# Sharing the attention transposes and V products among three heads instead of two, with a new order of the work

## The chip, the cores and the metric

The kernel runs on one core of a Trainium2 chip. A core has five engines with instruction streams of their own: TensorE (PE, matrix products, into PSUM), VectorE (DVE), ScalarE (ACT), GpSimd (POOL) and SyncE (SP). DMA engines move data between HBM and the on-chip SBUF; here SP and POOL issue the transfers. The metric is the time of one execution on the device in microseconds, as the median of several runs. Before the change it was 1774.65 us (three runs, 1773.49 to 1776.65).

## The reference

Two layers follow each other, twice: a recurrent attention (A) and a gated feed-forward network (B), each on a layernorm of its input with a residual sum. x has 2048 rows of 512; attention has 32 heads of 128, segments of 32 rows and 8 memory rows. All is bf16.

```python
for s in range(n_seg):                                  # 64 segments
    h = concatenate([mem, x[:, s*32:(s+1)*32]])         # 8 + 32 = 40 rows
    q, k, v = h @ Wq, h @ Wk, h @ Wv                    # per head, 512 -> 128
    scores = where(mask, q @ k.T * 128**-0.5, -1e9)     # 40 x 40 per head
    o = softmax(scores) @ v                             # 40 x 128 per head
    o = einsum('bhte,hed->btd', o, Wo)
    mem = o[:, :8]                                      # memory of the next segment
    outs.append(o[:, 8:])

def B(x): return (sigmoid(x @ w_gate) * (x @ w_up)) @ w_down   # 512 -> 1792 -> 512
```

The memory makes the 64 segments of one attention a chain: a segment needs the output of the one before it.

## The kernel before

**Steps.** The first and the second attention run interleaved. They are called jobs 0 and 1, and job 1 runs six segments behind (`LAG`). There are 70 steps (`emit_step`, L872). In 58 of them both jobs are at work and a matmul has 80 columns (two segments of 40 rows); in the first six and the last six only one is.

**Groups.** A step handles its 32 heads in six groups, five of six heads and one of two (`groups`, L512). A group has these stages: Q and K projections, three heads at a time (L949, 128x128 weight blocks against the 80 columns of `hT`); a copy to `qku` on ScalarE; scores (L984); mask, maximum, subtraction, exponential, sum and reciprocal on VectorE and ScalarE (L998 to L1012); the scaling into `pb` (L1015); the transposes of P (L1027); the copies that spread P^T into `ptsb` (L1032, issued at L1303 to L1313); the products with V (L1054); a copy to `otsb`; and the output projection (L1072), which adds up over all heads in one PSUM bank. The memory rows of that bank go to the next step's `hT` (L1085).

**Pairs of heads.** `pb` holds P of 80 rows (both jobs' queries) and, for each head, 40 keys at a pitch of 64. One transpose takes two heads, head u and head 16 + u: 80 x 128 in, 128 x 80 out, so that a head's keys lie on partitions 0 to 39 or 64 to 103. The spreading copies write the two heads into a block form: for each job 40 columns for the first head, with zeros below, and 40 for the second, with zeros above. The second copy covers partitions 0 to 103 and multiplies by a mask column `lower`, which is 0 on the first 64 partitions. One product then serves two heads of one job: V of both on 104 partitions as weights, 80 columns moving.

**V.** Rows of V that depend on x alone are computed ahead in big passes (`v_pass`, L739), written to a scratch tensor in HBM and brought into `vsb` (L918). Rows that depend on the memory are computed in the step as strips (`strips`, L863) and copied into `vsb` by DMA through `sst` (L929). A `vsb` tile holds two heads' rows (partitions 0 to 39 and 64 to 103) for 8 units; a step takes two tiles of a ring of three. Each job needs four transfers from scratch and four from the strips, on the SP queue.

**Feed-forward work.** `ffn` (L1127) runs once per block of four segments and job, from weights that POOL streams from HBM (L1166, L1167, L1191). These matmuls (L1174, L1197), the V passes and the layernorm transposes (L699, L1142) lie between the steps' own matmuls on TensorE.

**Order.** A `Planner` holds every task with a duration, its reads and writes, and buffer rings. It walks through modelled time and, on each engine, starts the ready task that comes first in a stored list (`SEQUENCE`). The order that results is the program order on each engine. Weight transfers on POOL also get a wait on a TensorE task that, by the model, ended before their planned start (L1282). Where TensorE's plan shows a gap of over 250 ns, `warm` (L447) puts in matmuls on the tile `hot` whose result nobody reads (L1297).

Of the kernel before, what the change touches and what calls it, by code (L numbers as in the profile page):

```python
# [20 lines left out]
P = 128  # L21
# [15 lines left out]
def mm_ns(n):  # L37
    return max(n / 2.4 + 2.5, 25.0)
# [14 lines left out]

SEQUENCE = r"""
;AsOsC|v+MjR9kLb}pcQnda7Mm$^5zu`zb?3;5sKz{Rmj5^3kR*HD{9a4C$pJ<wZm2fIZR%3?+XgW%;+b65$rzYj7ezK;wS2K8bkq`Ct3fbk0_8QV5#pP1SHH##{@E-}1p8b<v1c8}gL^qmgFuu=_Cmod@|aa)Bo
_(!7P{lowmZu!z=QxF6aTzb03ZNYwxWk94HP+-&b5ixb!rw7D&>->wAKE9p&fnHsC!#^79Oqv~2B~jFF>fB&4f|@_*cWiGdtUO{JV9YkvS4<gWKFzS_m2N;?Sd;nQLM*=$%E@Ib;(0pLg3_$2ZWJ(ljh!wN3NUs6
<5F&caLSK>)P*`J@~qpb;Y8L!JhX#{%taT;x!7FSEohnq5cBOK$g1sMwUcQ%dQwvAU?Yl(>+~FP4KnQw<4ai*m$Ni%@eF8yqWT`P6A}d&x}&%Y^h|Oi|C(c*m<{{{QKwuR?f4x6kfo7q7?!*PRo-`h^KDdYq}rrj
Qe}Cx;@>}6<vsP|nLHGVSR`?Jw!dwJc>$f)ug#YOjpt<QNggkYb%c$1L6x@M+krLbO%Xf*rWkO+VsgIXNF=S2DCNakULR0$_XnH*voY9g`Duym?=Qw1DQ1UX_&&DV1o7hG0of;$A4;6oHhlw3(-pf8u_$o1bCsWI
21H2wjjwk>ULoIcfwFF{{WIEcj}(P;nqh|W3C8W^?du{dVtsLV5j-;}!xpE5oI*H(-glbV!Xba!h~dqyDAH8Q{<?vpAWc@uL6XLV_}9<sCt_Ebk=m*)x3+Egk(=uP&?9cwL@07D#aRVqUGrpVxAd=yf@-RLiGaw6
NTi0vYZiE>0Jz9V9l9#&s)QY*9%mDFs#rqvM~Jhu_^M$OM||BbD$P%yrm;??MzxM}(n_{k35|H0!CF#hXp)ejb%omEhqh525X=MRzlUNqJHuH6gbaZ$g8&B-myDPo);n%pUHGq18&5~(vLdWo1&@32N*wJ)(P!Ig  # L60
YPsPtX;IoB6xc~Wc-NkP>>ENdzqQ+2CUI6{FdjQX`5%7%e&!W})4qbjHvwAFJ>Zu5A!7|={Tvw#<b4noq0Q=={ZkZKZe@GMEs@N?ba$8EB(cfCna5V`*IT<8XDYDd+^`?jTP<-T#4f%fWQ^+l2L$=eOhD&&Tg}A=
o(d^E0S^h*W|xu}v&))cVBD@UZWbc1Zw1IjVQ~PlGMjRS4AKjJ{J-sbNp=pfQ>-3Fk2-(OKqfc3p4Qj^EaLHuzfGs{9-yGY;d|Bx;#_AZWf<bcmcD^q<!SKv7?)hFHT0t%Q~Ob;8{_e5p8zrSM3j^V0UA6l<~K+8
qJ|0!*V%&_xZ?Yt0E*-(4@`PBKC3g~GEF#Bc|~h;7j1f6vH`IflKK?e=%?qkkvn1e5JhaZmOFlU%(5u0Hs>L24q5ucwhWIRX-C>7`rQn3M|q$jy$82}IedzD9{sy@`LTXSJIx~!QtE|YPh__?)`PR4g{$3s1>OV5
kDisZ#>ZOlso}JIu!@-+4!Xa38SYa{?+U=Bw;6sY6p`0LbH$jzPzrKd8tPZb8>Uz42l@9dwuVV2;J3K;Rd^B(QLO9R5o@Y09VHdike@DI^E<U=bp)K*-0_35QfiZphl*TxO*Kp%-e^ReuW6ObA7WMsi5I(MFW{9M
1uT02zVE=EO4@EIlq+WD<vErd+36l7K0Z@Z*FSV7eBIVW&36@5*u!b)pw|%zFj}iUdIXD1mw=5|{@Y!KJZKCqD^E9;$uf^%korHhU|Sh=Q)VdU_0xw<SU`{N#8#>p1|HgLVDlqta#Sh?l!HeP29lT+{K@`K<)Mp6
zA8Vk!f0UN)Mob;xoPeQ?aLl`XB1%3TKxhPkd1ImHK8+?j`l_Hr^fIiYB-k~c;tCC!<C&mOui!UI8wir)o}YA^zjX+T_Md853^_Qm}YAvo8j745^l`jABY;6$TnT{2+Ljr6v@(cC7L<>_*z-AP}(7Ay??OSs-Q8`
bieYOqR?{|n&&_>vmt{iqMTR+A<v)5iI}y9!m>&K>iQhOL|y@J&m0EBNk>GH^K^Z?QVHA_va0h}4*{Ea9t62I)*zXJ7EINdi{geJ$x1Wzfxr{lw{mYqw>T_Hz4cnHMF2;R1XC@VQL(0o1F)JmZO9dgG%zCVRCeu7
3p=-~+tO_ycon*Y6@-0<Ln!$dLO}z|P_(!`@VH>XlC(OE6LeIw)y{`npw!2HKI9v9t&pKXBZq>5Jd3UJ1H<hb04!s+Pf7V7fuXmw@4kGYFE6c7BJMjw=XPdb;8B1xd)odOI-6a9<FJY)Rwk}!ag=AwEwr}t8f!q{
aRtb8k)E}}o!S<cpj(8vjJI3#BM}N8I0s?`Z}=75QO3=rP^nPVA#^D7q;Vi&9T{;ZZIH8g0w6Gmg!+Kj<ca-aR+d>)XWl1BiDwb7xz~-2n*#-c`TgjGC-#l~G6uPi;|XKr=W+`bRu`+=nj{K8h>eL%VFe1ek4#7M
JU?IOJ)AusFVI8M2Zq0BU_1x<hVq!^{^3V!VL&!U&vOa&qBH74T11MaEy}NV1w+R@JqTM&nLl26)?Y(~#-2%Rz&frC^-Xule$T@g_(VrkgzgZEu!FN)NxJ-^d+nX$3!(z5BA`!*TOdvmcIWR5MpuHfxs2Gs6swfj  # L70
q{Ho52dpz2KT_Yy)ra>bx1ZUjA)M%A8nYiYbJ@vT_?keO&`A9qOHUa8g0ZWNP3`^#FSVBP!FgU)r}X6FA>&QW8qtKGR^}>NI&MCpavFu8?>y28LnF`0P?6`$P`I$jX-l@j!_H49T}>@yu_qe|i)>n7Q>|S#Rixw~
vUp*-H2v-mHL~^tYN43C{TKY}Ys7Y!N#|%4*_*xT!t={Y)sM(VOXDz^rE_Q>f}x4ruj%c9EYPFI^3=JA;b#NGq-W;<_@C~T>N^&6-XEF~(86+9{~i#5q5bdn6vF1mJ=#yX{q~DzNVc4^3qQh}Lj;U3DmZbc_7O^A
aO;tvP}@sNkkRhU>943-coTs&RS85wk`B07I$Rhfzk3xrXzrn=?H+2gfSXpkciJ}rHrJa#F>>5L4U1@pTAs}x&^ti4BM`U_c1w!<^4T*(I7-U4#WI%K%uLM^ka7BJ-gJvV%oaRPC-`dp0YI@53!yV(W(Bu;-hqk+
?gY7Ri?#O0Vybj{bLXQx%s5vml24M5`+5n_dwSc$|83*n`|)7ZvXRPSeU5qPOmyjO$AbYRG7mt~8hgQ|Ej7NVJ#*M!bDyI?b1NB@k+WQso&-iW2xY>xpw&`%)Qk@&c|eVHjrnajbCvTHBf6jEiqWy2B79ze8tLW^
Rm^<Q7rDKo?^#9DG=h)jZvB#$SNM_ZHB@AwmtqX1LqyHIcxQrTWvTgKRVLM*E9fcTKn-P}5LEjk*aCxa*uJmvk-&DP8XwO}TYHft!l3)u!;T%fetz4NZGa}EBeg0}n<K3P<V=WeqOgrsDc@u7FB<fomTQUji(l2^
r8rN)bo_gnWSReyFn*DP)QO~52c8C>ep^QTezVeAR^?wRP;fGCo2(^|Ey@J3L6VsyJ=-iDKXpE0)?Ip{jyZq|(uJb@7nGBi=leueOcIe@1MD=;ffKzH+sn|kpf=KW0TLbG5rzcXoq^l(!bGIn5Qo?pnXYJ4m5b)t
V&Xl^1Cdo>gy{^>LyVE{84PiLpza9^s~VP;vj8nyM#^{6klzZNL!<Np+yw)Ft0}m^3B0704|2^N=8b-;p1;MRE9PC7c&b`2h7?&biIx$r<}TIlyQm=^AJj({UU2yu`g<e#j&nvsM7#8gGc(xA0Lk~QgZ!$#GJ^Kv
hw%{Jv-&YY{A_AOcDIpMHn^foOT8G%xUP3!Jx5gKy>lWo6*}y>-|ujubGL`~oM6ZXUjsLxdb^nTM45mPo&+2ONt+8WZrWH3pRTu=GJB?_=dF2f?l{#{K%K+~s=CN@o=OK~X~8+;{29IXcND8wO3Qcj+BSOps~*JE
)IiAPY}L|2(?_FY#$mWq=2(vpVzXW1j6im<nD!~c#r}Is%`-N<>I0k-F^JUrjSpFz8z&$u#XBXv+qxEpN%;^g@EB#|6KwrOKzH!&n54%Atl~PL{GO|d4!wQl(d4FqOaLq$DeZyR0%PkMZki<;JF4|0g5H#?(UKN_
B5t~w{4v;)3H1aZi_jP@61_azKrAqo9yqT_uxHam(oPCqic3^f;ecc?awH$$`vR+BxWaCbD46a+4c+NY(JPgdZ-#G2Q98}020k_M@3xhycCo^}Zm3tLp-~67d$-`lww{bAacv*LfY$Zs6@NzB45n|7uiw!Frux4r  # L80
Vbk09oZ5N0mP~AYyX%F#|G~r<Atf>BV08~aQO1p)l?rgR7GMm%H)dnNKn9vJqOX99$>h>39P26|#`9rW);?dljEkmpM{u2hogN5h;rZZ*Au>p32Q`V$y|t+9Q$W<sqS}QYl{u9esG$#-P8I=;4T@YJjd~_CU3*y4
+CiwW$^1H=@=7|i;w{j-|4+gtXcwa?>n`I!|JrcM6DY{yD-d)RBaJSh<71r4q&0gLqSv`;NMPT~xQA%@iUvs5Siv@?5KV#rtFqAWh4tr`wjHBoI$2UHQ8Lpvtqm#VwJW%J{Yq=LCM*^{kPY5$9Od=&`s(}ZqguH5
u!DDl$u~uz9xYPTH_#7pwTLR!kXwg#5XK`KzJkX{S0{y0dLd)T0zc^0U&aeT!)hgua_8GT_>a-7C<s*c*~}?DF#3_Q>2J#+s8S7-!*DTO3*jx_eMid`9Jnotc8s*q&_iV!t>KYR<1}KKkuNg~$<u&_0Q4y-+Q7=K
h%N)X9196K9ZX1kbKh6Q+J2WO9?xH!g3#(}K{C)YnTJX2g+2z`DlF84q#dTb-8tO!DBAyIb5KKV^qKrII=L^7P9`gSk14=Et{Ep9_7_rlTen3Mu3T`6+IN;ZR`<rx!L(RBukVn^kgOAtXh8OXg}Yh^Bt(mljkb-H
=|Xc?Hzj<5sgLA&M7Pv2Hke=J^|)#kU%4j|<aUj#ez(_8X>T9j{Kv7(-V(C;h1W=bjz`Ka8<o54@E~nNCHZpTv@*LUSc8F}6bM*2Vm?98pIdwI;>c|+b5C1f0!LV)>X&5J%rlOn$PNF#blh#}Wk~cxn(+m3i-`un
%fDaxfsPGl=f;T#qQ^-jzTXRylZ5Gbp*EGz`WrI_mFx?8II}@~qBsSUfOU2$z$14e8p~>$U?1ACt@XijNvtKFdr9}x_csseTr{V%2ta!e;mLEhY)}6uYIbR&gkVV>h}!>+bYeV)!}$(Vi!;>YI%n>JcqQSRVS!ib
xXMw6U)dNTIob8uIiUMbGayImRvtI`lbhk5h*;h&@Vr{K{|vX+Di?yaE&&f->&%8toYize(iQx1w(l{xaKi$pCw!rOo0Wi|$NQJ`smOoW&INHohTt|`t2)5)uy@21FY3)YlzN)^*c(oqfP+EZx)D>X=$QF)5SY5J
3BfVrQqd-d9mp1d+*jiSi#W2Eo3}Oud-~&PpS`LzZ#5s2-KVtHzHReUp9TNB17#X~rp-BeiBEF#-VY-eUQ6Rjp+D`CEJe*n!tq*Lkv}FhCeDV8r$nB>=(h2H23;7tltIg`QJ&AC)U~hf?iy{X4L4E+Su4n!DA87j
u?U}5t~;?7xiC)v%aIca1dS6jR_InzL02buCkiX9Q${=N0q!+fH0WB$tm0CttsJ(esyW;ISr$d#ZlE&hBht^PxYk4L5XWS@Jj5U9-w0I2wVquBO5d;o!((=6K6REWaMIr@$m58J;nkc3$Ty;i@IDcLn-{BpLsvlE
g!)kIRhe&IQW6saRx$yE)N2v8DCV^o6}E9Mb&v}edu~~3Rd6~1$U5PbI74)1_=*k>PVT*mj>Ywra{`@$Ta3Qf@6*emC$KG4FEj>>vuE{IpE*~-wL;5;KzHauJrW%ZgU9l8d2eZ+v?uQzzLL0FK|86Y9&oy;z>juM  # L90
jX?x8E<GN*80{3;=}WRYJYK(19SRX<_GSp#>2_UI80^`sxExP=gL0?^S?S7fyNr4mQKg{Y-8dr~{L!Hf?mKEQcbb$1g|y{H4Bxp0*nGH$ku=E5{Lw-N=ucX<1Rfiy;38f_ewAFV+*2!XyB{-tUJrBeEO_a$uRdEV
T@VqKCldx(iq#N5vLcxiZaDm(JgDR{-{w7?uUTW5&q23MWn7)Z7mQB?coS@!I2h#QcM)_Nk?E;JH_-n?NdUn~#$@yr%I*B86;L><4DoL^p5o_|%{qHCNj^a3wC-OWCH1Yo?x$^UK}X>@AEUMsI<N&@?vYeV9)DiC
bVr$wqJnTzAK=y#R8BW9>(e0sAz%i$wQ(SS8Pka3N<=Eh6o_1$8+I%I$Co%x8j^>m$w>?9#-zkb?MTU2iy>_zEbTNtKjk^O#;-Hn&y&p6F0P8Up-dB^@wyTH&%HmK9;|>6cn5@B4_A7FUI7tG0ZL9bi_8MNR+Lvf
Ve9O8DIwrUXi&d;kbj=XMnUtlv86*vTNG-Kc~;b9QIph(oI%V$<7F@Bz56<2<Q=u#So@>CrTuK#C@4wIT#Kn7*)L1{GdFEbm9l7>f5w4>*guM5J7yd(!~ybSEg&%TE@SuPJZu-Q^I;r-5YTeNCOQV_J+}R1{{8-X
@baQz7MyJaMnfAHG_M@Nl9(lP6PL_?RFJe)JBCdu8;D1@*2~927___0Yn>eW6}b3CBC)fkp@8Di@)Jc)?Bqp9jbXnO%G&Zh9OcwEGV{sRi?sAvhZ}}%S!PFUlWpx<OX^vGLCSbMOL>*zZ_DgSV3Azq!hsYG9A!Sp
YY`FD^0jECcTDlW*^En{9metb#OzYkeV?89>sw`A9V}yzXIA?4B*S5+++k}JElYwDpP&|0^!}tb*nZPB?>WwhvJ^4r0r(G=h-4X?{aqsK_2V*rlFEj9N><^%X!~`dR(`>bscqFn7Z<;!#(_PidPUb))4LpRZlS(F
zfxdR?_f~HC1p;r+-qV|@W~TwX!M(4TaI3^F42u!1mS{xdymvE8QX>hLU1tYBQ(qkV<t~_Ju5vn_Ktx70={M3IZ-8DaIowumHXn8A_p(emJm}Z*INactOMp|i9!}kU}Vpq01MmctRSlq$v2aR^&CcYeYBiF$1`B|
# [1279 lines left out]
```

## Time and profile before

| what | value |
|---|---|
| median of three runs | 1774.65 us |
| profiled execution | 1778.1 us, its span 1776.3 us |
| TensorE busy | 1757.0 us, 40068 matmuls |
| VectorE, ScalarE, GpSimd busy | 1173.7, 1162.7, 576.2 us |
| transposes of P (L1027) | 1120, of 80 columns |
| products with V (L1054) | 2048, of 80 columns |
| copies into ptsb | 840, for 12 per step |
| transfers into vsb from scratch, from strips | 508, 516 |
| TensorE busy from 400 to 1600 us | 1195.98 of 1200 us |

Times in the profile are microseconds from the start of the span unless marked ns. "L949" is a line of the kernel. PEld is TensorE's loading of weights, which overlaps its matmuls; SPq is the queue that issues transfers. A group's row gives busy time and mean duration, then the idle time of its engine ahead of it and what ended that time. A single matmul lasts some 200 ns from start to end, but the next starts long before, so the distance between starts says what one costs. Durations in the prediction come from the profiled execution.

### The profile page before, as it was taken

Reading aid. Unit: us, or ns where it says so; the run is one execution under the profiler, and the core shown is the slowest. Engines: PE = TensorE matmul, PEld = TensorE weight load, DVE = VectorE, ACT = ScalarE, POOL = GpSimd, SP = SyncE. Lnnn points to the kernel's source line nnn. Section 1 sums busy time; section 2 is a strip of 40 time slices with the busy share of each in tenths; the row PEclk is TensorE's granted clock in tenths of the full one; section 3 lists DMA queues with packets and bytes.
Section 4 is the critical chain, followed back from the end, with each engine's and each line's share of the span. In section 5 each row is a group of like instructions: output and inputs, shape, how many; then the busy total and the mean of one; then the engine's idle time right before and its main releaser. Section 6 shows DMA issues by size and latency. Waiting matters only on the chain.

```text
span 1776.3 us, 92287 instructions
## 1 busy us (share of the span) xinstructions
PE 1757.0 (99%) x40068; PEld 1509.3 (85%) x40068; DVE 1173.7 (66%) x4044; ACT 1162.7 (65%) x2998; POOL 576.2 (32%) x833
## 2 busy tenths in 40 slices
PE   9999999999999999999999999999999999999998
PEld 4688788889888888989898898989888888889886
DVE  4376676777566567756776677657766766666675
ACT  6676767676666656766666667666666666666664
POOL 5413032513333242323334241333324232333432
PEclk9999999999999999999999999999999999999999
DMA  9835354734555464545556453555546444554543
GB/s 350 277 88 156 84 161 139 208 95 134 160 161 157 130 183 133 143 131 162 162 144 182 132 165 111 154 156 168 154 131 190 124 138 129 162 153 136 170 132 108
DMA packets 135289, 273.43 MB, mean 154 GB/s; under 512 B 30826, under 2 KB 68594, under 8 KB 134882
## 3 DMA queue, kind: packets, MB, share of 16 engines
q0 software_dynamic: 56512, 182.57, 35.1%
q1 hardware_dynamic: 78370, 84.96, 16.6%
q8 instruction: 314, 5.14, 1.3%
q14 instruction: 93, 0.76, 0.1%
HBM read 221.78 MB, written 27.07 MB: 140 GB/s over the span
## 4 chain that ended last, share of the span: by engine, by line
PE 93%; DMA 2%; DVE 2%; issue 1%; POOL 1%; ACT 1%; SPq 0%; POOLq 0%; ACTq 0%; DVEq 0%
PE bank L949 32%; PE bank L1072 16%; PE bank L1174 11%; PE bank L739 8%; PE bank L863 7%; PE bank L1197 5%; PE bank L984 4%; PE bank L1054 4%; PE bank L1027 2%; PE bank L699 1%; PE bank L1297 1%; DMA vsb<-sst 1%; PE bank L1142 1%; DMA wd<-in_B_w_down_dram 0%; POOL wu L1167 0%
## 5 line engine op out<-in xcount | busy, mean ns | idle before, releaser
L949 PE MATMUL bank<-hT,wq_sb 128*128 128x80 bf16 (+3 forms) x8960 | 615.5, 198 | 2.0 <-issue 1.5
L949 PE MATMUL bank<-hT,wk_sb 128*128 128x80 bf16 (+3 forms) x8960 | 614.8, 198 | 0.0
L1311 ACT CAST qku<-bank 128x480 bf16<-128x480 f32 (+4 forms) x770 | 387.6, 506 | 216.9 <-PE bank L949 179.5
L949 PEld LDWEIGHTS <-wq_sb 128*128 128x128 bf16 x8960 | 452.1, 99 | 22.7 <-issue 12.1
L949 PEld LDWEIGHTS <-wk_sb 128*128 128x128 bf16 x8960 | 446.8, 99 | 0.0
L998 DVE TENSOR_TENSOR st<-bank,cst 40x240 f32<-40x240 f32 (+3 forms) x768 | 278.0, 367 | 167.3 <-PE bank L984 160.3
L1072 PE MATMUL bank<-otsb,wo_sb 128*128 128x80 bf16 (+1 forms) x8960 | 359.9, 198 | 1.2 <-ACT otsb L1311 1.0
L1072 PEld LDWEIGHTS <-wo_sb 128*128 128x128 bf16 x8960 | 335.1, 99 | 15.8 <-issue 2.6
L1166 POOL DMA_DIRECT2D wg<-in_B_w_gate_dram x217 | 164.4, 757 | 310.4 <-PE bank L1174 102.6
L1311 ACT CAST otsb<-bank 128x480 bf16<-128x480 f32 (+3 forms) x420 | 198.5, 483 | 67.3 <-PE bank L1054 45.6
L1167 POOL DMA_DIRECT2D wu<-in_B_w_up_dram x217 | 163.7, 755 | 218.5 <-PE bank L984 81.0
L1191 POOL DMA_DIRECT2D wd<-in_B_w_down_dram x217 | 153.7, 708 | 209.1 <-PE bank L984 71.2
L1008 ACT ACTIVATE st<-st 80x240 f32<-80x240 f32 (+3 forms) x420 | 158.6, 381 | 35.5 <-DVE st L1005 32.5
L1010 DVE TENSOR_REDUCE small<-st 80x6 f32<-80x240 f32 (+3 forms) x420 | 150.9, 362 | 32.8 <-ACT st L1008 31.1
L1174 PE MATMUL bank<-xnT,wg 128*128 128x128 bf16 (+2 forms) x1784 | 171.6, 218 | 0.4 <-DMA wg<-in_B_w_gate_dram 0.4
L689 POOL TENSOR_TENSOR small<-small,cst 128x1 f32<-128x1 f32 (+1 forms) x80 | 44.6, 559 | 391.6 <-DVE small L688 386.6
L1174 PE MATMUL bank<-xnT,wu 128*128 128x128 bf16 (+2 forms) x1784 | 171.0, 218 | 0.0
L984 PE MATMUL bank<-qku 128*128 128x80 bf16 (+1 forms) x2240 | 162.3, 198 | 0.7 <-ACT qku L1311 0.7
L1005 DVE TENSOR_TENSOR st<-st,small 80x240 f32<-80x240 f32 (+3 forms) x420 | 153.9, 369 | 4.0
L1015 DVE TENSOR_TENSOR pb<-st,small 80x240 bf16<-80x240 f32 (+3 forms) x420 | 152.9, 369 | 3.8
L1003 DVE TENSOR_REDUCE small<-st 80x6 f32<-80x240 f32 (+3 forms) x420 | 151.1, 362 | 4.4
L1054 PE MATMUL bank<-ptsb,vsb 104*128 104x80 bf16 x2048 | 136.5, 199 | 3.5 <-DMA vsb<-sst 1.0
(106 smaller groups left out, 2396.2 us busy)
## 6 DMA issues: line engine op xcount, KB each, us to landing
wg<-in_B_w_gate_dram POOLq DMA_DIRECT2D x220, 256.0 KB, 4.3
wu<-in_B_w_up_dram POOLq DMA_DIRECT2D x220, 256.0 KB, 4.4
wd<-in_B_w_down_dram POOLq DMA_DIRECT2D x220, 256.0 KB, 4.3
vsb<-scr SPq DMA_DIRECT2D x460, 48.0 KB
vsb<-sst SPq DMA_DIRECT2D x464, 32.0 KB
scr<-vst SPq DMA_DIRECT2D x112, 96.0 KB
wv_sb<-in_A_Wv_dram SPq DMA_DIRECT2D x8, 512.0 KB
wo_sb<-in_A_Wo_dram SPq DMA_DIRECT2D x10, 384.0 KB
```

The source lines that it names most:

```text
L949: nc.tensor.matmul(o_ap, lhsT=W[:, c, h * P:(h + 1) * P], rhs=mv(c), start=(c == 0), stop=(c == DC - 1))
L984: nc.tensor.matmul(s_all(SB)[:, w0 + i, :], lhsT=fview(qku[:, i, 0, 0:1], [(1, P)]), rhs=qku[:, i, 1, 0:ncol], start=True, stop=True)
L998: pl.add("DVE", dve_ns(n, True), lambda gsz=gsz, hs=hs, st=st, SB=SB, pj_=pj_, npj_=npj_, mk=mk, idx=idx: nc.vector.tensor_tensor(out=st[p ...
L1005: pl.add("DVE", dve_ns(n), lambda gsz=gsz, hs=hs, st=st, mx=mx: nc.vector.tensor_tensor(out=st[pr, hs], in0=st[pr, hs], in1=mx[pr, hs].uns ...
L1008: pl.add("ACT", act_ns(n), lambda hs=hs, st=st: nc.scalar.activation(out=st[pr, hs], in_=st[pr, hs], func=ACTF.Exp, scale=self.scale), r=s ...
L1054: nc.tensor.matmul(fview(OB[:, o:o + 1], [(ncol, 2), (1, L)]), lhsT=self.vsb[halves[u // 8]][0:64 + L, j, (u % 8) * P:(u % 8 + 1) * P], rh ...
L1072: nc.tensor.matmul(WB[:, c * ncol:(c + 1) * ncol], lhsT=self.wo[:, h, c * P:(c + 1) * P], rhs=otsb[:, hl, 0:ncol], start=(h == 0 and c == ...
L1166: pl.add("POOL", 760, lambda wg=wg, fs=fs: nc.gpsimd.dma_start(out=wg[:], in_=self.wgv[:, :, fs]), r=[("wo", self.H - 1)], w=[gk] + bt, la ...
L1167: pl.add("POOL", 760, lambda wu=wu, fs=fs: nc.gpsimd.dma_start(out=wu[:], in_=self.wuv[:, :, fs]), r=[("wo", self.H - 1)], w=[uk] + bt, la ...
L1174: nc.tensor.matmul(gu[:, 2 * i + k, 0:n], lhsT=W[:, c, i * P:(i + 1) * P], rhs=xnT[:, c, rw], start=(c == 0), stop=(c == DC - 1))
L1191: pl.add("POOL", 760, lambda wd=wd, ip=ip: nc.gpsimd.dma_start(out=wd[:], in_=self.wdv[:, 2 * ip:2 * ip + 2, :]), w=[dk] + (["boot"] if se ...
L1311: nc.scalar.copy(out=dst, in_=src)
```

## The change

**Triples.** Heads 0 to 23 form eight units of three (u, 8 + u, 16 + u), heads 24 to 31 four units of two. The groups are now four with two triples (six heads), one with three pairs and one with one pair. `pb` has a pitch of 40, so a transpose takes 120 or 80 adjoining columns, and three heads' keys lie on partitions 0 to 119. The spreading copies are three for a group of triples, the second and third with mask columns `third[1]` and `third[2]`. A product of a triple has 120 partitions and 120 columns, of a pair 80 and 80.

**V tiles.** A step now takes one tile A (triples, 8 units) and one tile B (pairs, 4 units, half the width), from a ring of two each. Rows have a pitch of 40, so there are no gaps to clear. Each job needs five transfers from scratch and five from the strips, three of 8 heads and two of 4.

**Loads.** Wq, Wk and Wo are cut to suit the new groups; the first group needs nine heads of Wq and Wk.

**Order.** There is a new `SEQUENCE`. A second stored list, `TURNS`, fixes the order in which tasks take the `qku` buffers. The planner's constants change: 120 ns from a task to POOL, 465 ns (before, 205) after a TensorE task for the pace of weight transfers, 5.1 us (before, 4.7) for a weight transfer's landing, 114 ns (before, 80) for one small instruction.

**Places.** `hot` becomes part of `otsb[1]`, `negh` part of `small`.

```diff
+    TO_PE, TO_POOL, PACE = 32.0, 120.0, 465.0
...
+    def in_turn(self, pool):
+        own = [b.users[0] for b in self.bufs if b.users and b.pool is pool]
+        turn = [own[q] for q in unpack(TURNS, len(own))]
+        for a, b in zip(turn, turn[2:]):
+            self.tasks[b].deps.add(a)
...
-        for u in range(0, self.HH, 3):
-            us = list(range(u, min(u + 3, self.HH)))
-            self.groups.append(([h for k in us for h in (k, self.HH + k)], us))
+        for us in ((0, 1), (2, 3), (4, 5), (6, 7), (8, 9, 10), (11,)):
+            self.groups.append(([h for u in us for h in self.unit(u)], us))
...
+    def unit(self, u):
+        return [u, 8 + u, 16 + u] if u < 8 else [16 + u, 20 + u]
...
-        self.NV = 3
+        self.NV = 2
-        self.vsb = [c.tile([P, 2, 1024], BF16, name=f"vsb{i}") for i in range(self.NV)]
+        self.vsb = {("A", i): c.tile([P, 2, 1024], BF16, name=f"vsb{i}") for i in range(self.NV)}
+        self.vsb.update({("B", i): c.tile([P, 2, 512], BF16, name=f"vsb{self.NV + i}") for i in range(self.NV)})
-        self.pb = [c.tile([LW, HG, 64], BF16, name=f"pb{i}") for i in range(3)]
-        self.ptsb = [c.tile([P, HG, 2, L], BF16, name=f"ptsb{i}") for i in range(3)]
+        self.pb = [c.tile([LW, HG, L], BF16, name=f"pb{i}") for i in range(3)]
+        self.ptsb = [c.tile([P, 17 * L], BF16, name=f"ptsb{i}") for i in range(3)]
+        self.hot = fview(self.otsb[1][:, 0, 0:1], [(1, P)])
...
-        halves = [self.nxt("vsb", self.NV) for _ in range(2)]
+        vt = self.nxt("vsb", self.NV)
+        slots = [(("A", vt), i, 8 * i, 8) for i in range(3)] + [(("B", vt), i, 24 + 4 * i, 4) for i in range(2)]
...
-            for i4 in (0, 2, 1, 3):
+            for vh, i, h0, nh in slots:
...
+            w = gsz // nu
-                    nc.tensor.transpose(out=pt[:, ul * LW:(ul + 1) * LW], in_=pb[full, 2 * ul:2 * ul + 2, :].rearrange("p i k -> p (i k)"),
+                    nc.tensor.transpose(out=pt[:, ul * LW:(ul + 1) * LW], in_=pb[full, w * ul:w * ul + w, :].rearrange("p i k -> p (i k)"),
                                         identity=self.ident[full, full])
-            for i in (0, 1):
+            for i in range(w):
...
-                        nc.tensor.matmul(fview(OB[:, o:o + 1], [(ncol, 2), (1, L)]),
-                                         lhsT=self.vsb[halves[u // 8]][0:64 + L, j, (u % 8) * P:(u % 8 + 1) * P],
-                                         rhs=ptsb[0:64 + L, ul * nj + idx, :, :], start=True, stop=True)
+                        nc.tensor.matmul(fview(OB[:, o:o + 1], [(ncol, w), (1, L)]),
+                                         lhsT=self.vsb[vh][0:w * L, j, u % 8 * P:(u % 8 + 1) * P],
+                                         rhs=ptsb[0:w * L, 3 * L * (ul * nj + idx):3 * L * (ul * nj + idx) + w * L], start=True, stop=True)
...
-        ends = [tk.start + tk.dur + self.pl.LAT["PE"] for tk in pes]
+        ends = [tk.start + tk.dur + self.pl.PACE for tk in pes]
```

## The prediction

> **What bounds the kernel now.** I read the page's engine shares first, then the chain that ended last, then its pieces in order of time, then the groups by form, then the timeline of a step with one job.
>
> ```profile
> span 1776.3 us, 92287 instructions
> PE 1757.0 (99%) x40068; PEld 1509.3 (85%) x40068; DVE 1173.7 (66%) x4044; ACT 1162.7 (65%) x2998; POOL 576.2 (32%) x833
> PEclk9999999999999999999999999999999999999999
> ...
> PE 93%; DMA 2%; DVE 2%; issue 1%; POOL 1%; ACT 1%; SPq 0%; POOLq 0%; ACTq 0%; DVEq 0%
> ```
>
> TensorE is busy for 99% at full granted clock, and the chain runs through it for 93%. VectorE and ScalarE have about 600 us of room each. So the price of an edit is what it does to TensorE's row of matmuls, and next to that what it does where TensorE has nothing to do. Pieces of the chain (start us, us, what) give the rhythm:
>
> ```profile
> 603.14 0.22 PE bank L1054 x6
> ...
> 606.98 0.89 PE bank L1174 x16
> ...
> 612.61 0.86 PE bank L949 x24
> ...
> 617.34 0.11 PE bank L1027 x3
> ```
>
> 24 matmuls of 80 columns take 0.86 us, 35.8 ns each; 16 of 128 columns (L1174) take 0.89, 55.6 each: 0.41 ns a column and some 2.5 ns each. Transposes (L1027) and products with V (L1054) keep that rhythm (36.7 in both, rounded). Weight loads are hidden behind the matmul before them. The groups of loads by form (busy us, mean ns) show one more thing:
>
> ```profile
> L1054 PEld LDWEIGHTS <-vsb 104*128 104x128 bf16 x2048 | 102.7, 98 | 18.6 <-issue 6.4 <-DMA vsb<-scr 0.2
> L1027 PEld LDWEIGHTS <-pb 80*128 80x128 bf16 x1120 | 69.1, 98 | 15.4 <-DVE pb L1015 2.0 <-DVE st L998 0.4
> L776 PEld LDWEIGHTS <-xvl 128*64 128x64 bf16 x64 | 3.3, 109 | 3.4 <-ACT wd L1311 0.4 <-issue 0.4
> L863 PEld LDWEIGHTS <-xvl 128*32 128x32 bf16 x64 | 1.5, 96 | 1.9 <-issue 0.4 <-ACT xvl L1311 0.2
> L1197 PEld LDWEIGHTS <-hff 128*96 128x96 bf16 x14 | 1.3, 122 | 2.0 <-DVE hff L1180 1.2 <-issue 0.4
> ```
>
> A load of 32 columns takes 96 ns, of 64 109, of 96 122: 0.41 ns a column. One of 128 columns takes 98, no more than one of 32. Full loads are fast, short ones pay for every column.
>
> **Part one, the transposes.** A step transposed 16 pairs; it will transpose 8 triples and 4 pairs, always with 80 columns moving. Over 70 steps 280 of 1120 go: 280 x 35.8 ns = 10.0 us less, all of it on the path.
>
> But the stationary operand of a transpose is P itself, and its width falls from 128 columns (two heads at a pitch of 64) to 120 or 80. By the slope a load of 120 columns streams for 120 x 0.41 = 50 ns, and the 80-column matmul before it covers 33. The trace has one such place: at 1755.74 us a 96-column load (40 ns) follows a matmul of the 25 ns rhythm, and the matmul behind it lasts 396 ns where the next lasts 379: 17 ns stick out, as the sum says. I count 17 ns for the second triple of each group, which follows the first. The first follows other work: over the timeline 59% of the runs of transposes stand behind 80 columns, 29% behind 128 or 512 (0 exposed), the rest behind shorter ones (25 ns): 12.6 ns on average. 70 x 4 groups x (17 + 12.6) = 8.3 us more. The 80-column loads of the pairs stream 33 ns and stay covered. Bounds: 0 if such loads are hidden, 14 us if each shows 25 ns. I take 8.3, since the 96-column case is nearest.
>
> The Trainium skill speaks against the change here: "TensorE: Matmul & The Clock Gate", section on weight-path perf modes, says that the fast load is on only with 128 weights of a type other than FP32. Its section on LDWEIGHTS prices a plain load at columns / 1.2 ns, 100 ns for 120 columns; by that estimate the exposed time would be some 34 us and the kernel would end near 1793 us. The rows above agree with the first and show half of the second, 0.41 ns a column.
>
> **Part two, the products with V.** Per job and step 16 matmuls of 80 columns become 8 of 120 (120 x 0.41 + 2.5 = 52.5 ns) and 4 of 80. 128 job-steps x (16 x 35.8 - 8 x 52.5 - 4 x 35.8) = 128 x 9.6 ns = 1.2 us less. Only the fixed part is saved. Their loads stay 128 wide.
>
> **Part three, spreading P into the block form.** A group of six heads in triples has one plain and two scaled copies of 160 elements for one and one of 240. From the rows of the copies (ScalarE 459, 360, 325 ns scaled and 347, 246, 213 plain for 240, 120, 80; VectorE 331, 270, 247 and 268, 205, 184): 160 elements take about 392 and 280, and 289 and 226. Mixed as now, 0.73 us becomes 0.97: +0.24 us x 232 groups, and +0.23 x 48 groups with one job, 67 us over both engines. Other TensorE work covers it at 65% use; without that cover 67 us would be the price, and where TensorE waits for this group alone it is some 0.2 us.
>
> **Part four, ten transfers for eight.** The strips' issues (median 587 ns on SP) and those from scratch (355 ns) grow by two each in a full step: 1.9 us more of SP's 25 us. Behind them queue the scratch writes, x loads and stores. SP waits 349 us in all for L1054 before L918, because three half buffers hold one and a half steps; two whole sets hold two, so the same queue loses much of that wait. In a full step I price this at nothing: the first product stands some 9 us behind its strips (L863 at 609.59, L1054 at 620.63). In a step with one job it shows:
>
> ```profile
> 107.09 1.91 PE L863 MATMUL bank<-wv_sb,hT 128*32 128x512 bf16 x32
> ...
> 109.66 3.55 SPq L929 DMA_DIRECT2D vsb<-sst  x4
> ...
> 112.61 0.65 PE L1297 MATMUL bank<-hot 128*128 128x512 bf16 x3
> ...
> 113.21 0.97 PE L1297 MATMUL bank<-hot 128*128 128x512 bf16 x4
> ...
> 114.34 0.38 PE L1054 MATMUL bank<-ptsb,vsb 104*128 104x80 bf16 x6 [0.16 <-issue]
> ```
>
> Filler matmuls (L1297) stand where nothing useful is ready, and the first product waits for the strips of the first half, two issues. Now it waits for three, 0.57 to 0.89 us later (four issues in 3.55 us here, two in 1.15 in the next step). Three steps (102 to 136 us) have such fillers: 3 x 0.73 = 2.2 us more. Bounds: 0 if other work is put there, 12 x 0.89 = 10.7 us if all steps with one job pay.
>
> **Edits at nothing.** The gap clears (three of 1.89 us on ScalarE) go and the ptsb clears grow, both under the boot's fillers and V passes; uncovered, 5.7 us less to 0.6 more. The first group needs nine heads of Wq and Wk for six, 0.79 MB at 372 GB/s, 2.1 us: those loads are issued from 7 us on and first used at 48; uncovered +2.1. The filler operand moves into otsb1, so a filler can wait for that copy, 0 to 0.36 us (240 elements) at twelve places in the chain. Two reductions for the masks are paid in the boot.
>
> **Part five, the order.** Nothing in the trace shows it. What it can win is TensorE's idle 19.3 us, less 1.0 at the start and 4.8 in the last 16 us, plus 5.6 us of fillers between 85 and 218 us: 19.1 us. What it can lose I bound by 10 us: as much again as the chain loses between 100 and 160 us (fillers 6.4%, issue 4.7%, POOL's weight issues over 6%, so some 17% of 60 us). There the planned landing of weights (4.7 to 5.1 us) and the pace of POOL's issues (205 to 465 ns) act, in the helpful direction. I take a third of the 19.1, 6.4 us less.
>
> **Sum.** -10.0 + 8.3 - 1.2 + 2.2 - 6.4 = -7.1 us: 1771.0 for the profiled execution (1778.1, span 1776.3) and 1767.5 against the median of 1774.65, which lies 3.5 below it.
>
> **Rivals.** *Loads hidden:* if loads of 120 columns cost no rhythm, or transposes stand behind long matmuls, 8.3 us come back: 1759.2. For it: 29% already stand so; against it: the 17 ns.
> *The order wins nothing:* -0.7 in all, 1774, no change. For it: the middle of the run (400 to 1600 us) has only 4 us idle.
> *Slower:* the third strip transfer gates the first product in all twelve one-job steps, 10.7 us for 2.2, with no gain of the order: 1774.65 - 2.9 (parts one and two) + 10.7 = 1782.4. It decides above 0.54 us a step ((2.9 + 3.55) / 12), if the order wins nothing. For it: the timeline above; against it: the last six steps show few fillers.
>
> **How the numbers follow.** Forecast with the order's gain 0.45, own range 1761 to 1771; loads hidden, under 1761, 0.17; no change 0.16; slower 0.22. A measurement tells 0.2%, 3.5 us, from nothing. Faster 0.62, same 0.16, slower 0.22. The range of 1757 to 1782 reaches past the hidden loads and to the slower rival, and leaves out about 2 in 10.
>
> **What would show it.** Transposes 840 in number, 560 of their loads 120 wide at about 132 ns, about 52 ns between two triples; 1536 products, 1024 of them with 120 columns; spreads about 67 us dearer; fillers and idle from 85 to 220 us. Loads of 98 ns at 120 columns, or two triples 36 ns apart, refute part one. A changed idle in the middle of the run would make the prediction wrong from the order alone.

## The result, and the profile after

The changed kernel takes 1790.12 us (median of four runs, 1788.38 to 1794.11) where the kernel before takes 1775.35 in the same sitting: 0.8% slower, ratio 1.0082, 95% interval 1.0067 to 1.0097. Forecast were 1767.5 us, a range of 1757 to 1782, and "faster". The profiled execution took 1789.87 us. Its page:

```profile
span 1788.0 us, 91153 instructions
PE 1752.0 (98%) x39103; PEld 1512.2 (85%) x39311; DVE 1182.3 (66%) x4076; ACT 1179.3 (66%) x3243; POOL 578.6 (32%) x837
PEclk9999999999999999999999999999999999999999
...
PE 89%; ACT 3%; DVE 2%; issue 1%; SPq 1%; DMA 1%; POOL 0%; DVEq 0%; ACTq 0%; POOLq 0%
```

TensorE shows 5 us less busy time than before, in a span that is 11.7 us longer, and the chain runs through it for 89% instead of 93%. The records of 208 of its matmuls are missing (39103 for 39311 weight loads), so part of the 5 us may be theirs; but waits did grow. The groups by form (busy us, mean ns of one | idle before them) show the weight loads that the prediction spoke of:

```profile
L1067 PEld LDWEIGHTS <-pb 80*120 80x120 bf16 x560 | 55.7, 134 | 9.6 <-DVE pb L1054 1.9 <-DVE st L1044 0.4
L1067 PEld LDWEIGHTS <-pb 80*80 80x80 bf16 x280 | 22.2, 118 | 4.2 <-DVE pb L1054 0.9
L1096 PEld LDWEIGHTS <-vsb 120*128 120x128 bf16 x1024 | 65.5, 98 | 15.7 <-issue 4.6 <-DMA vsb<-sst 0.3
```

A load of 120 columns takes 134 ns (132 were forecast), and one of 128 columns 98, though it has more rows (120 for 80).

Adding up, for each kind of matmul, the distances from one start to the next in the two traces gives where the path changed (each missing matmul is counted where its weight load stands). Transposes fall from 46.2 us to 41.2, products with V rise from 80.5 to 82.9, V passes from 146.2 to 152.2, and fillers from 25.0 to 30.8 (94 to 129 matmuls); what is left adds some 2 us, and the sum is 11.6 us. The start of each step's strip tells when: the strip of step 1 starts at 89.3 us before and at 97.2 after, 7.9 us late. Up to 1500 us the lag stays mostly between 6 and 10, and the last strip is 11.8 us late. So the boot (all that comes before the first steps) lost 8 us, the long middle gave nothing back, and the end lost a little more.

In the boot two rows of ScalarE's waits stand out (15 to 62 us; us in total, times, longest):

```profile
ACT wg L1354 <- DMA scr<-wg: 5.5, 1, 5.5
ACT wd L1354 <- DMA scr<-wd: 4.7, 1, 4.7
```

The boot copies V rows out of PSUM into a ring of nine buffers (the wg, wu and wd tiles), from which they are written to scratch. ScalarE waits for a buffer whose write has not landed, and the timeline of the second wait (start us, us, engine, what) shows how it reaches TensorE:

```profile
53.03 1.03 PE L778 MATMUL bank<-wv_sb,xvf 128*128 128x512 bf16 x3
...
55.90 0.58 ACT L1354 CAST wd<-bank 128x512 bf16<-128x512 f32 x1 [4.70 <-DMA scr<-wd]
...
56.38 0.59 ACT L1354 CAST wg<-bank 128x512 bf16<-128x512 f32 x1
56.86 0.25 ACT L1354 CAST kx<-bank 128x84 bf16<-128x84 f32 x1
56.98 0.47 ACT L1354 COPY xvf<-bank 128x128 bf16<-128x128 bf16 x1
...
57.51 1.46 PE L778 MATMUL bank<-wv_sb,xvf 128*128 128x512 bf16 x3 [3.45 <-ACT xvf L1354]
```

The copy into xvf is short and ready, but it stands in ScalarE's queue behind the copy that waits. TensorE is idle for 3.45 us for it. Before, the longest such wait of ScalarE was 0.7 us.

The wait has a second price. Two stretches of this time (from and to in us, length, busy us of PE, PEld, DVE, ACT and POOL, granted TensorE clock, DMA share, GB/s), in the changed kernel and then before:

```profile
56.00:58.00 2.00, 0.49 (x2) 0.22 (x3) 0.00 (x0) 1.88 (x5) 0.73 (x2) 0.75 1.05 356
58.00:62.00 4.00, 4.00 (x31) 1.79 (x30) 0.41 (x1) 1.45 (x3) 1.92 (x4) 0.70 0.93 338
```

```profile
56.00:58.00 2.00, 2.00 (x19) 1.07 (x18) 0.52 (x1) 1.17 (x2) 1.12 (x2) 1.00 1.11 307
58.00:62.00 4.00, 4.00 (x22) 1.61 (x24) 0.21 (x1) 2.41 (x5) 1.63 (x3) 1.00 1.03 361
```

From 57.0 to 60.4 us the granted clock is 0.50, and matmuls of 512 columns start some 427 ns apart where they otherwise start 216 apart: 1.4 us more. So of the 6.0 us by which the V passes grew, 4.5 are two waits (3.45 and 1.0 us) and 1.4 this clock.

A step with one job answers to the step that the prediction showed:

```profile
114.65 1.91 PE L902 MATMUL bank<-wv_sb,hT 128*32 128x512 bf16 x32
117.22 4.29 SPq L968 DMA_DIRECT2D vsb<-sst  x5
...
120.60 1.94 PE L1340 MATMUL bank<-otsb 128*128 128x512 bf16 x9
...
122.38 0.48 PE L1096 MATMUL bank<-ptsb,vsb 120*128 120x120 bf16 x6
```

From the strip's start to the first product it is 7.73 us, 7.25 before: 0.5 us more, about what the forecast put on the third transfer. Fillers stand right ahead of the product in both, so whether the transfer or the fillers set it is not shown, and the strips' lag does not grow in these steps (7.9 us at step 1, 7.8 at step 5).

### The profile page after: what moved, and what is told of

The parts are those of the page before. It is cut to its first block, busy times and chain, and to the rows that moved or that the text cites. A ratio compares the mean times of both kernels' runs of the same rounds, so it can differ in the third digit from the quotient of the medians.

```text
span 1788.0 us, 91153 instructions
## 1 busy us (share of the span) xinstructions
PE 1752.0 (98%) x39103; PEld 1512.2 (85%) x39311; DVE 1182.3 (66%) x4076; ACT 1179.3 (66%) x3243; POOL 578.6 (32%) x837
## 4 chain that ended last, share of the span: by engine, by line
PE 89%; ACT 3%; DVE 2%; issue 1%; SPq 1%; DMA 1%; POOL 0%; DVEq 0%; ACTq 0%; POOLq 0%
PE bank L988 32%; PE bank L1114 17%; PE bank L1216 10%; PE bank L902 7%; PE bank L778 6%; PE bank L1023 4%; PE bank L1096 4%; PE bank L1239 4%; PE bank L1067 2%; PE bank L738 1%; DVE st L1037 1%; PE bank L1340 1%; SPq L968 1%; ACT ptsb L1346 1%; PE bank L1184 1%
## 5 line engine op out<-in xcount | busy, mean ns | idle before, releaser
L1354 ACT CAST qku<-bank 128x480 bf16<-128x480 f32 (+3 forms) x770 | 380.7, 507 | 215.5 <-PE bank L988 185.1
L988 PEld LDWEIGHTS <-wq_sb 128*128 128x128 bf16 x8960 | 453.4, 99 | 23.3 <-issue 11.7
L1346 ACT ACTIVATE ptsb<-bank,small 80x160 bf16<-80x160 bf16 (+5 forms) x477 | 169.5, 379 | 27.7 <-PE bank L1067 23.9
L728 POOL TENSOR_TENSOR small<-small 128x1 f32<-128x1 f32 (+1 forms) x80 | 44.8, 563 | 402.1 <-DVE small L727 400.0
```

The source lines that it names most:

```text
L988: nc.tensor.matmul(o_ap, lhsT=W[:, c, h * P:(h + 1) * P], rhs=mv(c), start=(c == 0), stop=(c == DC - 1))
L1346: nc.scalar.activation(out=dst, in_=src, func=ACTF.Copy, scale=by)
L1354: nc.scalar.copy(out=dst, in_=src)
```

## The experiments

All were timed beside the kernel before on one chip per group of runs. That kernel's median moved between 1774 and 1778 us over the groups, so ratios are compared, not times. Line numbers shift by a few lines from kernel to kernel.

**The changed kernel again**, as the measure for its neighbours.

> The changed kernel itself, beside the runs of this call, so that they are read against it on the same chip: 1790 to 1793 us, some 0.8% above the kernel before.

Measured: 1794.3 us against 1777.2, ratio 1.0106 (1.0091 to 1.0120), somewhat worse than in the first sitting. The products' waits for V rows are larger here (4.6 us in the trace for 2.2), which matters below, and the mean granted clock was 0.998 in three of the four runs for 0.999 in all four of the first sitting.

**Full weight loads.** pb's tiles are laid next to constants, so that a load can run eight columns over:

```
-  in_=pb[full, w * ul:w * ul + w, :]           # 120 or 80 columns
+  in_=pbw[:, w * L * ul:w * L * ul + m]        # m = 128 but for a group's third pair
```

> The transposes of P in the groups of three read 128 columns of pb instead of 120 (the eight columns behind a head triple are constants or the next tile's, and the eight extra rows of the result are not read), and two of the three in a pair group read 128 instead of 80. Order, spreads, products and transfers stay. Theory (a weight load of fewer than 128 columns is slow and shows): the 120-column loads, 134 ns each in the changed kernel, become about 108 ns like the full ones, the 560 transposes behind them go from a mean of 52.0 ns to 36 to 41, which is 6 to 9 us less: 1781 to 1784. Rival (the loads lie under other work, and the transposes are spaced by something else): the spacing stays at 50 ns and the time within 2 us of 1790.

Measured: 1788.2 us, ratio 1.0058 (1.0040 to 1.0075). The loads, by form:

```profile
L1071 PEld LDWEIGHTS <-cst 80*128 80x128 bf16 x770 | 57.5, 99 | 15.8 <-DVE cst L1057 3.5 <-issue 0.8
```

With eight columns more a load takes 99 ns in place of 134 (108 were expected). The transposes' sum falls from 41.2 us to 36.7. That sum holds a few long waits; the distances under 200 ns fall from a mean of 47.1 ns to 39.0, which is 6.8 us over 840. In groups of two triples the first shows 50 ns behind 80-column work and 40 behind longer work, and 40 to 42 with full loads; the second shows 55 or 45, and 35 with full loads (medians). So the theory holds for the spacing. By the ratios the time falls by 4.3 us against the first sitting and 8.5 against the second. The profiled execution is the slowest of the six (1795.2 us): its products waited 5.9 us for V rows from the strips, where the first profile of the changed kernel shows 1.8, its V passes 5.5 us for one copy, and the clock was at 0.50 for 6.8 us from 56.2 and for 3.4 us from 1694.6.

**The table's load early.** The removed gap clears were ScalarE's first instructions, so the load of its table came with them at 0.74 us; in the changed kernel it stands in front of the first copies of the V passes.

```
   nc.vector.memset(self.negh, -0.5)
+  nc.scalar.copy(out=self.third[1], in_=self.negh)
```

> The changed kernel with one small ScalarE copy put ahead of everything, so that the load of ScalarE's table (1.28 us, at 0.74 us before and at 13.56 us in the changed kernel, in front of the first copies into xvf) comes early again. Theory (the removed gap clears had carried the table load; the boot passes the delay on): the first V pass starts 1.3 to 1.9 us earlier and the end follows: 1788 to 1789. Rival (what bounds the boot is the transfers, so a late start of the V passes is taken up at the next wait for a buffer): the first V pass is early, step 0 is not, 1790.

Measured: 1800.3 us, ratio 1.0123 (1.0106 to 1.0141), no gain. The first V pass did start earlier (14.21 us in its timeline, 16.44 in the changed kernel), yet the strip of step 0 stood at 73.67 us, against 72.5 and 72.89 in the two profiles of the changed kernel. ScalarE waited longer instead:

```profile
ACT wd L1355 <- DMA scr<-wd: 7.0, 1, 7.0
```

The rival holds: an earlier start is taken up at the next full buffer. That its ratio is even 3 us above the worse one of the changed kernel is in part the clock: its trace has it at 0.50 for 6.8 us from 55.1 (TensorE was idle for the first half of this) and for 3.4 us from 304.2, with waits for V rows of 1.6 and 1.3 us, where the changed kernel's trace has the one stretch of 3.4. The rest was not settled.

**Two more boot buffers.** The order stays as planned; only the ring grows by two halves of a vsb tile.

```
   order = self.pl.plan()
+  self.bootp.tiles = self.bootp.tiles + [self.vsb[("A", 1)][:, i, :] for i in (0, 1)]
+  ...   # buffers dealt out anew, the longest free one first
```

> The changed kernel with eleven instead of nine buffers for the boot's V rows (two halves of a vsb tile that is not used before step 1 join the ring); the order of every engine stays. Theory (ScalarE's waits of 5.5 and 4.7 us at 41 and 56 us are waits for a buffer whose write to scratch has not landed, and TensorE loses 1.0 and 5 us behind them): both waits shrink or go, the strip of step 0 starts 4 to 6 us earlier, time 1784 to 1786. Rival (the transfers as a whole are late, weights included, since the DMA engines are full from 10 to 60 us): the wait moves to the next transfer, and the time stays within 2 us of 1790.

Measured: 1793.7 us, ratio 1.0088 (1.0073 to 1.0103). The boot did as the theory says: V passes lost 2.2 us against their rhythm of 216 ns instead of 6.6, the clock stayed at 1.00, and step 0 started 4.5 us earlier. ScalarE still waits 5.4 and 1.6 us for buffers, but TensorE only 1.5 us behind it. (All seven traces of the new order with nine buffers have the stretch at 0.50 between 55 and 63 us; of the eleven with more, one has such a stretch in the boot, from 43.1 us, with a wait of 3.46 us.) At the end nothing of it was left: the strips' lag grew from 4.5 us at step 1 to 12.9 at the last. By itself the boot's gain does not reach the end. That later waits of the products for V rows take it up is the likely reason (their waits between 290 and 1590 us are 5.9 us here, 1.3 before), not shown by this run alone.

**Pairs in the new order.**

```
   def ptr(...):
+      if w == 3: three transposes of 80 columns; return
   def pvm(...):
+      if w == 3: three products per job, rhs 80 wide; return
```

> The changed kernel with its order, transfers, weight loads and three spreads kept, but in the groups of three triples' work is done as three transposes of 80 columns and products of pairs (80 wide) as before; the products take V rows of the wrong heads, so this prices time alone. Theory (sharing in threes saves some 8 us of TensorE's time, and the loss lies in the order and the boot): transposes 840 x 41 ns for 560 x 52 (+5 us), products 1536 x 37.7 ns for 1024 x 53 (+3 us): 1795 to 1799. Rival (sharing in threes is itself what does not pay): 1788 to 1792.

Measured: 1798.5 us, ratio 1.0115 (1.0096 to 1.0135). The time of the theory, but against the changed kernel's 1.0082 and 1.0106 only 2 to 6 us more, so by itself this run is not decisive.

**Eight transfers for ten, and two spreads for three.**

```
-  pl.add("SP", 632, lambda ...: nc.sync.dma_start(
+  pl.add("SP", 632, lambda ...: None if t > 7 and vh[0] == "A" and i == 2 else nc.sync.dma_start(
```

> The changed kernel with the strip's transfers into the third place of the first eight heads left out from step 8 on (two of ten in a step of two jobs, one of five in a step of one), so that group 0's product waits for four transfers, as before, not six; the V rows there go stale, so this prices time alone. Order and everything else stay. Theory (the two transfers more, issued one after another by SyncE, make the wait of the first product for its V rows longer): the waits of the products for vsb from the strip's tile go from 1.8 us, and 5 to 6 us in two of the runs, to under 1 us, and the time falls by 2 to 5 us. Rival (the order leaves room for them, as forecast): within 1.5 us of the changed kernel.

> The changed kernel with the third spread of each group of triples left out (the third heads' P is zero then, so this prices time alone); order and everything else stay. Theory (the third spreads, some 190 ns each on ScalarE or VectorE, lie beside other work, as forecast): within 1.5 us of the changed kernel. Rival (they are behind the longer waits for qku, pb and ptsb in the middle): TensorE's lost time between 290 and 1590 us falls from 28 towards 22 us, and the time by 3 to 6 us.

Measured: without the third place's transfers 1788.1 us, ratio 1.0063 (1.0051 to 1.0075); without the third spread (its function returns at once for i = 2) 1794.6, ratio 1.0093 (1.0080 to 1.0106). Beside the changed kernel's 1794.3 that is 6 us (8 by the ratios) and nothing clear of the intervals. TensorE's waits for V rows, in the changed kernel and then without those transfers:

```profile
PE bank L1096 <- DMA vsb<-sst: 2.7, 3, 1.6
PE bank L1096 <- DMA vsb<-scr: 1.9, 1, 1.9
```

```profile
PE bank L1096 <- DMA vsb<-sst: 0.3, 1, 0.3
```

All but 0.3 us of 4.6 is gone, and what the products lose between 290 and 1590 us against their rhythm falls by 5.2 us. The third spreads lie beside other work, as forecast.

**Loads and buffers together.**

> The changed kernel with the 128-column weight loads and the two more boot buffers together. Theory (both losses are real and add up: 5 to 7 us of transposes, 3 to 4 us of the boot): 8 to 10 us under the changed kernel, 1781 to 1783 beside a kernel before of 1776. Rival (what TensorE gains is given back at the next wait for V rows, as the two more buffers alone seemed to show in the middle): 3 to 5 us under the changed kernel.

Measured: 1784.3 us, ratio 1.0046 (1.0032 to 1.0060), 10 us under the changed kernel, as the theory says for two losses that add up. The changed kernel was not timed in the sitting of the two single edits, so the sum is tested to some 4 us only, the distance between the changed kernel's own two sittings.

**All three causes out, and then only the order left.** The first takes the 128-column loads, the two buffers and the eight transfers together. The second has the eight transfers and the buffers, but the pairs on TensorE.

> The changed kernel with the 128-column weight loads, the two more boot buffers, and the strip's transfers into the third place left out from step 8 on (V rows go stale there, so this prices time alone). Theory (three separate causes that add up): the 10 us of the first two and the 6 us of the transfers together, 1777 to 1779 beside a kernel before of 1777, ratio 1.000 to 1.002. Rival (they overlap, since what TensorE gains at one wait it gives back at the next): 1782 to 1784, no better than the first two alone.

> The changed kernel with the work of TensorE brought back to that of before (three transposes of 80 columns and products of pairs for the groups of triples), eight transfers of the strip in place of ten from step 8 on, and the two more boot buffers: what is left of the change is mainly its order, with the plan of its boot, its tail and the third spread (V rows of wrong heads and stale ones, so this prices time alone). Theory (the order, forecast to win 6.4 us, costs time): 5 to 10 us over the kernel before, ratio 1.003 to 1.006. Rival (the order is neutral or better, and the loss was all in loads, buffers and transfers): ratio 0.997 to 1.001.

Measured: 1776.0 us, ratio 0.9996 (0.9987 to 1.0005), and 1787.3 us, ratio 1.0062 (1.0049 to 1.0075). These two settle most. In one order and with the same transfers, threes with full loads are worth 0.66%, 11.7 us, against pairs. And with the work of before on TensorE (the transposes take 44.9 us for 46.2, the products 81.0 for 80.5), the new order and what comes with it are 11 us slower than the old one. What comes with it: the third spreads, which cost nothing by themselves, two more transfers from scratch, the boot's edits and the fillers' operand. The two profiled executions lie 8.0 us apart. By the strips, 2.7 us of that are there at step 1, 4.3 at 1606 us and 7.6 at the last strip; between 400 and 1600 us TensorE is idle for 3.7 us, 4.0 before. So the cost stands in the boot and in the last steps. Fillers, which stand where the plan itself has gaps, show it too: 14.4 us for 11.2 in the first 20 us, and 3.2 for 1.4 from 1700 us on.

**The first product later.** In 53 of 70 steps it goes behind up to 1.2 us of TensorE's work that was ready by the plan:

```
+  order = self.later(order, pes, pace)   # moves the product of group 0, and what depends on it
```

> The changed kernel with the 128-column loads, the two more boot buffers, and in 53 of the 70 steps the first product moved behind up to 1.2 us (0.4 us in the mean) of TensorE's work that was ready anyway, so that its six transfers have that much longer to land; nothing is left out. Theory (the waits for the fifth and sixth transfer cost 5 to 6 us in all): 2 to 4 us under the 1.0046 of the loads and buffers alone, ratio 1.002 to 1.0035. Rival (the later product makes what hangs on it late): ratio 1.0046 or more.

> As the kernel with the later first product, and the boot's start as before: one small ScalarE copy ahead of everything, so that the table is loaded at some 0.7 us, and the first four loads of x issued ahead of mem0 and of the first load of wq. Theory (with buffers to spare the boot passes an earlier start on): the first V pass 2 to 3 us earlier, step 0 and the end 1.5 to 3 us earlier than without. Rival (as with the early table alone, the boot is set by transfers and nothing comes through): no gain.

Measured: 1811.8 us, ratio 1.0193 (1.0174 to 1.0212), and 1812.2 with the boot's start changed as well, ratio 1.0196 (1.0176 to 1.0215). The rival, and by far. The waits of the first of them:

```profile
PE bank L1120 <- ACT otsb L1401: 9.6, 23, 0.7
PE bank L1100 <- DMA vsb<-sst: 4.1, 5, 1.7
PE bank L1100 <- ACT ptsb L1393: 3.6, 3, 2.1
```

The product's copy into otsb now comes late in ScalarE's queue, and the next matmuls with Wo wait for it 23 times. The trace also has the clock at 0.50 for 3.4 us twice, from 302.7 us, with waits of 1.7 and 2.1 us, and from 1620.2. A mean shift of 0.4 us of one task in a step cost some 26 us against the 1.0046.

**A second queue for the third place.**

```
-  nc.sync.dma_start(
+  (nc.scalar if vh[0] == "A" and i == 2 else nc.sync).dma_start(
```

> The changed kernel with the 128-column loads and the two more boot buffers, complete, and with the strip's transfers into the third place (two of the six that the first product waits for) issued by ScalarE in place of SyncE. Theory (the wait is for issues that SyncE makes one after another, 0.65 us apart: the sixth goes out 4.2 us after the strip, where the fourth went out at 2.7): the last of the six goes out at 2.7 us or so, the products' waits for vsb fall as they did with these transfers left out, and the time goes to 1777 to 1780, ratio 1.000 to 1.002. Rival (128 issues and their waits delay ScalarE's copies of qku and otsb, on which TensorE waits next): no better than the 1.0046 of loads and buffers alone, or worse.

Measured: 1777.0 us, ratio 1.0016 (1.0007 to 1.0025). The gain of the theory. The waits for V rows go:

```profile
PE bank L1100 <- DMA vsb<-sst: 0.3, 1, 0.3
```

The expectation's 4.2 us is the sixth transfer of any kind. In most steps transfers into tile B, for which the first product does not wait, stand between or ahead of the six into tile A. Told apart by their size (32 KB, the others 16), the last of the six starts 6.2 us after the strip's end in the changed kernel (median of 51 steps between 290 and 1590 us), 5.95 with loads and buffers alone, and 4.9 here; one step in ten has it at 8.2 us or later with loads and buffers alone, at 6.6 or later here. So the last one does go out earlier, by 1 us, though not at the 2.7 that was expected. Whether it also lands sooner after its issue is open, since the traces do not show when SyncE's transfers land. (Here too late boot rows could overwrite V rows of step 1.)

**The same complete, then one more buffer.** From here every row stands.

> 128-column loads, the third place's transfers by ScalarE, and the two more boot buffers used only until the transfers of step 1 go into the same tile (in the runs with two more buffers so far, a late boot row could overwrite some V rows of step 1, so those price time alone; here every row stands). Theory (the waits of the boot that cost lie before 57 us): the time of the run with the late rows, ratio 1.000 to 1.002. Rival (the late buffers carried part of the gain): 1.002 to 1.005.

> The same with a third more buffer, from the vsb tile of step 1's other heads. Theory (every buffer more takes a wait for a write to scratch away, and the boot is still some 4 us late): 1 to 3 us less than with two, ratio 0.999 to 1.001, which would be the first at or under the kernel before. Rival (what is left of the boot's 4 us is the order's own plan, the transfers' total): within 1 us of two buffers.

Measured: 1779.1 us, ratio 1.0005 (0.9996 to 1.0014), and 1778.2, ratio 1.0003 (0.9994 to 1.0013). A third buffer halves what is left of the boot's lag (4.2 us at step 1 against 2.1), and the time is the same within the intervals: the rival, for the time.

**Fillers off otsb, and the boot's start.**

```
+  hot = self.hot if tk.start < 8000.0 else self.ident
...
-  nc.tensor.matmul(B[:, 0:m * P], lhsT=self.hot, ...
+  nc.tensor.matmul(B[:, 0:m * P], lhsT=hot, ...
```

> The complete kernel with three more buffers, and the fillers after the boot reading the identity in place of otsb's second buffer, for whose copies seven of them waited 2.9 us. Theory (as forecast, the shared buffer costs nothing: the fillers stand in gaps that the order leaves anyway): within 1 us of three buffers alone, ratio 1.000 to 1.001. Rival (a filler that starts late ends late, and the product behind it with it): 1.5 to 3 us less, ratio 0.998 to 0.9995.

> The same, with the table loaded at the start and the first loads of x ahead of mem0 and wq. Theory (the boot is set by its transfers; an earlier first V pass is taken up at the next wait, as with the early table alone): within 1 us of the run without, step 0 not earlier. Rival (with eleven and more buffers nothing takes it up): step 0 and the end 2 to 3 us earlier, ratio under 0.999.

Measured: 1775.2 us against 1777.6, ratio 0.9986 (0.9977 to 0.9995), and 1775.2 with the early start, ratio 0.9986 (0.9978 to 0.9995). The fillers' waits, in the kernel with three more buffers:

```profile
PE bank L1357 <- ACT otsb L1371: 3.0, 7, 0.6
```

With the identity as operand that row is gone, and the time falls by about 3 us: the rival. The last edit shows little: its first V pass starts at 15.40 us, only 0.16 earlier than without, so this run did not get the early start that it was made for. The kernel with free fillers is the best of the study, 2.4 us faster than the kernel before; it keeps the threes and the new order, with full loads, three more buffers and two transfers on ScalarE's queue.

## Why the prediction was wrong

**The order is the step that failed first.** It was put at 6.4 us less, with losses bounded by 10. With TensorE's work and the strips' transfers as before, the new order and what comes with it cost 11 us, about 3 of them, by the run with free fillers, the fillers' operand. The forecast looked for losses between 100 and 160 us; they stand in the boot and in the last steps. Which part of the order makes them (the sequence, the buffers' turns, the planner's constants) stays open. The bound was a share of a chain in another kernel; nothing in a trace of before shows what an order that is not there will do. The rival "the order wins nothing" was too kind, and the rival "slower", which came nearer to the time, had another reason: the third transfer in the steps with one job.

**The boot had no term for its ring of buffers.** The prediction costed the edits of the boot one by one at nothing, "under the boot's fillers and V passes". Of the gap clears that was right as far as it was tested: the table's load moved with them and made the first V passes late, but the run that put it back and started them 2.2 us earlier gained nothing, since the boot was held by writes to scratch. What it missed is that ScalarE waits twice for a buffer of the ring in the new boot, and that TensorE's clock halves with the second wait. With eleven buffers ScalarE still waits, but TensorE loses little by it and keeps its clock; with twelve ScalarE's own waits are 0.3 us at most. So the ring is shown to be the cause; that the new order of the boot's copies and weight loads brings them on is likely, not shown. Two more buffers took 3.4 us of the 7.9 at step 1 away; a third took 2 more off the lag, without a gain in time that the intervals show.

**Ten transfers for eight was priced in the wrong steps.** In steps with one job 0.5 us were seen, near the forecast, and the lag did not grow by them. In full steps the prediction counted on 9 us between strip and first product and took nothing. The trace after has 10.5 us there in the median, and the product still waits in some steps; leaving two transfers out gave 6 to 8 us, and a second queue 5. The median gap was the wrong number to read. In the changed kernel's second profile four waits, the longest 1.9 us, make up 4.6 us, and the last of the six transfers starts 6.2 us after the strip in the median, but 7.9 us or later in one step of ten.

**The fillers' operand** was bounded by "0 to 0.36 us at twelve places" and taken at 0. It cost about 3 us, within the bound, in seven waits of 0.43 us in the mean: fewer than twelve, and longer than the 0.36.

**The transposes were right in kind.** 280 fewer, 560 loads of 120 columns at 134 ns for 132 forecast, a spacing of 50 ns in the median for 52 forecast between two triples. Count and loads together were put at 1.7 us less. The sum fell by 5.0, but half of this is shorter waits (distances of 200 ns and more make 4.5 us before and 1.9 after); the distances under 200 ns fell by 2.4. The loads' share was 8.3 us in the forecast, and full loads take 6.8 us off these distances. What was too high is the first triple of each group: 7.4 ns in the mean for 12.6. The second shows some 16 for 17. The Trainium skill, "TensorE: Matmul & The Clock Gate", says in its section on weight-path perf modes that the fast load wants 128 columns; the rows of 134 ns at 120 columns and 99 at 128 agree. The price for a plain load in the page's section on LDWEIGHTS, columns / 1.2 ns, from which the prediction worked out an end near 1793 us as an estimate, comes close to the measured time for another reason: the loads account for about 7 us of it.

**The products** were put at 1.2 us less and came out 2.4 more, because of waits. One of 120 columns takes 52 ns in the median, for 52.5 forecast; the distances under 200 ns fell from 76.0 us to 74.3, and what is longer rose from 4.5 us to 8.6. In the best kernel the whole sum is 77.4.

**The spreads** were hidden, as forecast.

The sum, by ratios: the new order with what comes with it costs some 11 us at the work of before, the sharing gains 11.7 with full loads, and short loads, the ring and the two transfers cost 15 to 20 on top (1.0082 and 1.0106 against 0.9996). The change's idea was worth what its count of matmuls says (10.0 + 1.2 us). It was lost in the order and in four places beside it: the loads, nearly at their forecast price; the transfers and the fillers' operand, named and priced at nothing; and the ring, which had no term.

## What to carry to other kernels

When an edit takes work off the bound engine, look for what it asks of the queues beside it (how many transfers the next product waits for, how often a ring is turned), and read their late tail, not their median. An order that is new as a whole can't be credited with a gain from the idle time of the old one: keep its gain at zero with room on both sides, and test it apart from the work. Where TensorE waits, look at the granted clock behind the wait as well. And keep a stationary operand at its full 128 columns even if the last ones are rubbish that nobody reads.

## What was not expected of the hardware

- Reading eight columns more makes a weight load faster: 99 ns for 128 columns, 134 for 120, 118 for 80 (80 rows in all three).
- A transfer issued by ScalarE takes 515 ns of its queue in the median, one by SyncE 587, and 129 of them on ScalarE cost nothing that the time shows: beside loads and buffers alone the ratio fell from 1.0046 to 1.0016, and TensorE's waits for V rows, 4.6 us in the changed kernel, were 0.3.
- A start of the V passes that was 2.2 us earlier did not make step 0 earlier: with the DMA engines at full share in every slice of 5 us from 10 to 55 us of that run, a wait for a buffer took it up.
- With a wait of TensorE of 2.2 to 5.7 us in the boot the granted clock fell to 0.50 for 3.4 us, in two runs for 6.8. Not with every such wait: one of 3.3 us in the run with the second queue left it at 1.00.
